# Linear attention and a channel mix on one core: the first load of q split by head pairs, zeros and a product moved ahead, and a new order of steps

## The chip, the cores and the metric

The kernel runs on 1 core of one Trainium2 chip. The metric is device time in microseconds. The median of three runs before the change is 200.35 us (200.12, 200.35 and 202.0).

## The reference, cut to what matters

Batch 8, 8 heads, 576 tokens, head size 64; so 512 channels, and 1024 in the hidden layer. Everything comes in as float32 and goes out as float32.

```
kv   = einsum('bhsd,bhse->bhde', k, v)            # 64x64 per head
out  = einsum('bhsd,bhde->bhse', q, kv)
rms  = sqrt(mean(out*out, axis=-1) + 1e-6)
x    = (out / rms * g_norm), heads side by side    # [8, 576, 512]
x_prev = x shifted by one token, zero at token 0
xk   = mu_k * x + (1 - mu_k) * x_prev              # xr alike with mu_r
k    = max(xk @ w_k, 0)                            # 512 -> 1024
v    = (k * k) @ w_v                               # 1024 -> 512
r    = sigmoid(xr @ w_r)                           # 512 -> 512
result = r * v
```

## The kernel before

The kernel works in bfloat16 with channels on the partitions. For each batch it forms k'v per head, turns q so that channels lie on partitions, multiplies the two into PSUM (`u`), squares the result on ScalarE, takes the mean over a head with a product by a block matrix on TensorE (`ms`), takes the inverse root on ScalarE (`rs`) and multiplies on VectorE (`mu`) into x. Then x_prev - x (`d`, for the first two batches `dc`), its products with 1 - mu (`sc`), and the sums xk and xr (`add`; `fu` does both in one step). Then come xk w_k (`K`), its relu out of PSUM (`Ko`) and its square (`ks`), xr w_r (`R`) with its sigmoid (`S`), the square times w_v (`V`, two halves), the product of both (`fin`) and the store (`st`). Pairs of batches share the buffers of xr and of the squares, so a 128-row tile of R and V covers 128 of 1152 tokens.

**The order is written out by hand.** All steps of all batches stand in one string, `ORDER`, of words like `uc.0.1=6`. The loop at the end of the kernel takes the words one after the other, looks the name up in a table (`ops`), and calls it with the numbers behind it; the digits after `=` are the PSUM banks that it takes (eight banks, 0 to 7); a trailing `'` puts a step that can run on VectorE or ScalarE on VectorE. Tile's scheduler is off (`tc.manual_schedule()`), so each engine runs its steps in the order of the string, and waits of one engine for another follow from the data and the buffers. The output buffers are a pool of six (`fin`, L601; `bufs=6`). The queues to know:

- POOL (GpSimd) issues every load that turns float32 into bfloat16: `lf` (a part of k, v or q of batch 0 or 1, L200; arguments batch, which of k v q as 0 1 2, head pairs from and to, columns from and to), `lw` (a part of w_k, w_r, w_v as 0 1 2, L221), `ld` (k, v or q of a later batch, L200, L212 and L214). `gt` copies one column of turned q, so that POOL waits until q of that batch has been turned.
- SP issues the first k and v of head pairs 0 and 1 without a cast (`lraw`, L188; then `cast`, L246 or L248, on ScalarE or VectorE), the rows of mu and g (`lrow`, L192 and L194), turns of q for batches 2 and on (`qd`, L362 and L364), turns of y for batches 5 and on (`yd`, L421) and the stores (`st`, L618).

**The front, batches 0 and 1.** `set.0` zeroes and fills small constants; `set.1` makes the identities; `set.2` writes zeros over the block forms of k'v (`kv_heads`, `kv_pairs`, L271), which batches 2 and on need. `wm.n` runs n products of zeros (L253), whose result nobody reads. `kc` (L302) is k'v for a range of head pairs, and `kco` its copy out of PSUM; `qc` (L313) turns q by products with the identity, `qco` copies it out (L246 or L248); `uc` (L324) multiplies a piece; `sq`, `ms`, `rs`, `mu` (L435, L439, L444, L463) are as above. Batch 0 is cut into seven pieces: 0, 1 and 2 are head pairs 0, 1 and 2 of columns 192 to 576, pieces 3 and 4 the two halves of these columns of head pair 3, and 5 and 6 the columns 0 to 192 of pairs 0 and 2, and of 1 and 3. `col` turns the rows of mu and g into columns (L467, L470, L471), which every `mu` and `sc` reads. `wrap` (L476) copies the last tokens of x ahead of the first ones. For batch 0 the product with w_k is done for the columns 256 to 576 first (`Kf`, one 128-channel block of the hidden layer and a range of head pairs, L531; `Kfo` out of PSUM), and for the columns 0 to 256 later (`Kl`, two blocks, L542; `Klo`). `ksp` squares parts of it. `tab` loads ScalarE's table for roots (0) or sigmoids (1).

In the order before, q of batch 0, columns 192 to 576 of all four head pairs, is one load, and the first on POOL's queue. The first word of the products with R comes ahead of `Kl`, and `set.2` comes after the last add of batch 0.

Of the kernel before, what the change touches and what calls it, by code (L numbers as in the profile page):

```python
# [30 lines left out]
    add.0.0.0.0.256 Kf.5.0.4.256=5 Kf.0.3.4.256 Kfo.0.256 Kfo.4.256 Kfo.5.256 lw.0.3.0.4.6.8 Kf.6.0.4.256=6
    Kf.7.0.4.256=1 Kfo.1.256' Kf.2.2.3.256 Kf.2.3.4.256 sc.0.0.3.0.256 Kfo.6.256 Kfo.7.256' add.0.0.1.0.256
    set.2 lf.1.2.0.4.0.576 qc.1.0.2.0.576=47 wm.2=5 qc.1.2.4.0.576=56 qco.1.1.0.576 qco.1.3.0.576 qco.1.2.0.576
    lw.1.0.0.4.0.4 R.0.1=0 R.0.0=7 S.0.0 Kfo.3.256' R.0.2=1 S.0.2 lf.1.0.0.4.0.576 R.0.3=6 S.0.3 Kfo.2.256'
    ksp.0.4.256.576' Kl.0.256=5 qco.1.0.0.576 Klo.0.256' Kl.3.256=3 Klo.3.256' lf.1.1.0.2.0.576 kc.1.0.2=27
    kco.1.1' lf.1.1.2.4.0.576 kc.1.2.4=16 kco.1.3' S.0.1 tab.0.1 kco.1.0 uc.1.1=4 ksp.4.8.256.576' kco.1.2'
    Kl.2.256=5 sq.1.1 ms.1.1=0 uc.1.5=3 uc.1.3=7 uc.1.2=2 sq.1.5 uc.1.0=6 Klo.2.256' ksp.4.8.0.256' rs.1.1
    mu.1.1 Kl.1.256=1 Klo.1.256' ksp.0.4.0.256' sq.1.3 sq.1.2 ms.1.5=5 rs.1.5 mu.1.5 sq.1.0 lw.2.0.0.4.0.4
    V.0.3.0=0 ms.1.2=4 rs.1.2 mu.1.2 ms.1.3=5 rs.1.3 mu.1.3 V.0.2.0=1 uc.1.4=4 sq.1.4 ms.1.0=3 rs.1.0 mu.1.0
    lw.2.1.4.8.0.4 V.0.3.1 ms.1.4=5 rs.1.4 mu.1.4 V.0.1.0=2 V.0.1.1 wrap.1 dc.1.0.2.0.576 V.0.2.1 ld.1.2  # L40
    dc.1.2.4.0.576 ld.0.2 sc.1.1.0' sc.1.1.3' V.0.0.0=3 V.0.0.1 sc.1.1.1 add.1.1.0 sc.1.1.2 add.1.1.1 R.1.6=7
    fin.0.2 sc.1.0.0 sc.1.0.2 ld.2.2 sc.1.0.3 sc.1.0.1 ld.2.3 fin.0.1 R.1.5=5 tab.1.1 S.1.5 kv.2=64 kvo.2.3
    qd.2.0 R.1.7=1 gt.2 add.1.0.0 add.1.0.1 K.1.3.1=2 K.1.2.0=5 fin.0.3 Ko.1.2.0' K.1.3.0=0 kvo.2.0' kvo.2.1'
    kvo.2.2 R.1.4=4 S.1.4 kvo.2.4' K.1.6.0=5 K.1.2.1=6 Ko.1.3.0' qd.2.1 qd.3.0 K.1.7.1=0 kvo.2.5' Ko.1.3.1'
    Ko.1.2.1' K.1.0.0=4 ks.1.2 K.1.7.0=2 R.1.8=6 fin.0.0 Ko.1.7.0' S.1.6 Ko.1.6.0 S.1.7 S.1.8 tab.0.2 st.0.2
    Ko.1.0.0' K.1.5.0=3 Ko.1.5.0' K.1.6.1=7 K.1.0.1=2 Ko.1.0.1 ld.1.3 Ko.1.7.1' ks.1.7' K.1.1.0=5 Ko.1.6.1
    ld.0.3 K.1.1.1=4 ld.0.4 Ko.1.1.0 Ko.1.1.1' ks.1.3' K.1.4.0=1 Ko.1.4.0 ld.1.4 K.1.5.1=6 u.2.1=30 u.2.2=2
    u.2.0=74 ld.2.4 ld.0.5 ld.1.5 ks.1.1' Ko.1.5.1' ks.1.5' ks.1.0 sq.2.3 sq.2.0 ks.1.6' K.1.4.1=5 Ko.1.4.1'
    ks.1.4' ms.2.3=1 rs.2.3 sq.2.2 mu.2.3 st.0.1 V.1.8.0=6 ms.2.0=5 V.1.8.1 sq.2.1 qd.3.1 ms.2.2=1 rs.2.0
    V.1.7.0=0 mu.2.0 rs.2.2 mu.2.2 fin.1.8 st.0.3 ms.2.1=5 rs.2.1 sq.2.4 V.1.4.0=1 V.1.6.0=7 mu.2.1 d.2.0 d.2.4  # L50
    ms.2.4=3 rs.2.4 mu.2.4 d.2.1 d.2.2 d.2.3 sc.2.1.0' qd.4.0 gt.3 sc.2.0.0 sc.2.0.2' sc.2.0.1' sc.2.1.1'
    V.1.7.1 add.2.1.0 V.1.5.0=5 V.1.5.1 sc.2.1.3 sc.2.1.2 tab.1.2 kv.3=64 kvo.3.3 kvo.3.1 kvo.3.0 kvo.3.2 gt.4
    V.1.6.1 qd.4.1 V.1.4.1 add.2.1.1 R.2.3=3 R.2.0=2 fin.1.5 fin.1.4 R.2.1=5 S.2.0 kvo.3.5 S.2.1 fin.1.6 st.1.8
    add.2.0.0 R.2.2=6 st.0.0 st.1.6 st.1.5 zl sc.2.0.3' kvo.3.4' S.2.3 add.2.0.1 fin.1.7 u.3.1=41 sq.3.2 kv.4=72
# [24 lines left out]
    ks.4.5' tab.1.5 mu.5.4 K.4.4.0=4 Ko.4.4.0' K.4.3.1=6 Ko.4.3.1' K.4.7.0=5 K.4.6.0=0 K.4.4.1=1 K.4.7.1=3
    K.4.6.1=7 ks.4.3 ks.4.1' V.4.1.0=4 V.4.3.0=6 Ko.4.4.1' Ko.4.7.0 Ko.4.7.1 kvo.6.5' ut.6.0=1 gs.5.0 kvr.6.0'  # L80
# [639 lines left out]
```

## Time and profile before

| what | us |
|---|---|
| median of 3 runs | 200.35 |
| the profiled execution, its own time | 200.72 |
| its span, first to last instruction | 198.9 |
| TensorE busy | 188.9 |
| VectorE busy | 156.7 |
| ScalarE busy | 144.5 |
| mean granted TensorE clock, as a share | 0.996 |
| first product with w_k (L531) starts | 17.08 |
| first product with w_r (L576) starts | 24.69 |
| first product with w_k of batch 1 (L556) starts | 45.5 |

The profiled execution is one run, recorded; its time of 200.72 us is its span and what lies around it. Times in the profile are from the start of the span. PE is TensorE's products, PEld its weight loads, DVE is VectorE, ACT ScalarE, POOL GpSimd, SP the sync engine. A line of a timeline gives the start, the length, the engine, the line of the kernel and the operation with what it writes and reads; in brackets stands how long the engine had been idle before it, and what ended that. A row of a group of equal instructions one behind the other is one line with its count. A chain of waits follows the work that ended last back to its start.

### The profile page before, as it was taken

The page shows a single profiled execution, that of the slowest core. Times are in us where ns is not written, and L with a number is a line of the kernel's source. Part 1 is how long each engine was busy: PE and PEld are TensorE (multiplying, and loading weights), DVE is VectorE, ACT ScalarE, POOL GpSimd, SP SyncE. Part 2 cuts the span into 40 slices and gives each one's busy share as a digit, 9 for nine tenths or more (in the row PEclk, how much of TensorE's full clock was granted, in tenths as well). Part 3 has the DMA queues.
Part 4 walks back from the last instruction along what each step waited for, and adds up shares of the span by engine and source line. Part 5 has one row for each costly group of instructions (what it writes and reads, how often), then busy time and mean ns, then how long its engine had stood idle before and what let it go on. Part 6 is the DMA issues. An engine that isn't in the chain of part 4 may idle for free.

```text
span 198.9 us, 4745 instructions
## 1 busy us (share of the span) xinstructions
PE 188.9 (95%) x1879; PEld 111.4 (56%) x1900; DVE 156.7 (79%) x348; ACT 144.5 (73%) x280; POOL 32.6 (16%) x54
## 2 busy tenths in 40 slices
PE   7879899999999999999999999999999999999991
PEld 2444556446745476545764477645764666476541
DVE  1259978998689988988799987996898788969242
ACT  3188868695995889989875997969798858528330
POOL 8485141001920000730005000000000000000000
PEclk9999999999999999999999999999999999999998
DMA  6999999999999999899997999519460126104154
GB/s 218 178 198 203 207 206 208 205 194 160 155 247 228 204 204 196 158 198 212 198 237 131 234 184 105 176 72 230 80 187 21 53 53 167 47 0 158 58 185 132
DMA packets 49547, 32.24 MB, mean 162 GB/s; under 512 B 25836, under 2 KB 44532, under 8 KB 49524
## 3 DMA queue, kind: packets, MB, share of 16 engines
q0 software_dynamic: 22672, 16.19, 54.8%
q1 hardware_dynamic: 26692, 15.61, 33.6%
q8 instruction: 15, 0.25, 0.5%
q10 hardware_dynamic: 160, 0.13, 0.3%
q14 instruction: 8, 0.07, 0.1%
HBM read 33.56 MB, written 9.44 MB: 216 GB/s over the span
## 4 chain that ended last, share of the span: by engine, by line
PE 70%; DMA 14%; DVE 9%; issue 2%; POOL 1%; ACT 1%; SPq 0%; POOLq 0%; DVEq 0%
PE ps_v L586 26%; PE ps_km L556 24%; PE ps_r L576 12%; DMA wr_sb<-in_moe_w_r_dram 6%; DMA out_dram<-out_sb 4%; DMA q<-in_q_dram 4%; DVE rt L520 3%; PE ps_km L542 2%; PE ps_ms L439 2%; DVE xT L463 2%; DVE xk L511 1%; PE ps_kv L338 1%; PE ps_u L392 1%; DVE out_sb L601 1%; PE ps_v L594 1%
## 5 line engine op out<-in xcount | busy, mean ns | idle before, releaser
L586 PE MATMUL ps_v<-wv_sb,sqk 128*128 128x512 bf16 x270 | 64.7, 379 | 0.8 <-issue 0.2
L556 PE MATMUL ps_km<-xk,wk_sb 128*128 128x288 bf16 x448 | 60.4, 286 | 0.1
L556 PEld LDWEIGHTS <-wk_sb 128*128 128x128 bf16 x448 | 43.2, 98 | 15.2 <-issue 0.8
L586 PEld LDWEIGHTS <-sqk 128*128 128x128 bf16 x280 | 26.9, 98 | 29.5 <-DVE sqk L526 0.9
L520 DVE TENSOR_SCALAR rt<-ps_km 128x288 bf16<-128x288 f32 (+2 forms) x65 | 29.1, 466 | 8.3 <-PE ps_km L556 6.2
L576 PE MATMUL ps_r<-wr_sb,xr 128*128 128x512 bf16 x136 | 32.8, 379 | 1.2 <-DMA wr_sb<-in_moe_w_r_dram 0.4
L601 DVE TENSOR_TENSOR out_sb<-ps_v,sig 128x512 f32<-128x512 f32 (+1 forms) x37 | 24.1, 669 | 8.3 <-PE ps_v L586 2.7
L518 ACT ACTIVATE rt<-ps_km 128x288 bf16<-128x288 f32 (+1 forms) x59 | 22.5, 410 | 10.3 <-PE ps_km L556 10.0
L581 ACT ACTIVATE sig<-ps_r 128x512 bf16<-128x512 f32 x36 | 20.9, 598 | 11.5 <-PE ps_r L576 7.1
L500 ACT ACTIVATE m<-dx,cols 128x576 bf16<-128x576 bf16 (+1 forms) x28 | 19.7, 757 | 6.2 <-DVE dx L483 2.6
L463 DVE SCALAR_TENSOR_TENSOR xT<-ps_u,cols,rs 128x512 bf16<-128x512 f32 (+4 forms) x31 | 19.0, 626 | 4.5 <-ACT rs L444 4.3
L576 PEld LDWEIGHTS <-xr 128*128 128x128 bf16 x144 | 13.6, 98 | 15.8 <-DVE xr L511 1.0
L444 ACT ACTIVATE rs<-ps_ms,eps 128x512 f32<-128x512 f32 (+4 forms) x31 | 18.2, 595 | 2.9 <-PE ps_ms L439 2.7
L648 ACT ACT_TABLE_LOAD x15 | 19.2, 1283 | 0.3
L526 DVE TENSOR_TENSOR sqk<-rt 128x576 bf16<-128x576 bf16 (+2 forms) x35 | 16.7, 488 | 1.7 <-ACT rt L518 0.9
L524 ACT ACTIVATE sqk<-rt 128x576 bf16<-128x576 bf16 x25 | 16.5, 680 | 1.6 <-DVE rt L520 1.3
L435 ACT ACTIVATE sq<-ps_u 128x512 bf16<-128x512 f32 (+4 forms) x31 | 14.8, 499 | 1.9 <-PE ps_u L324 0.8
L367 POOL COPY gates<-qT 128x1 bf16<-128x1 bf16 x5 | 1.3, 264 | 74.8 <-DMA qT<-in_q 74.8
L502 DVE TENSOR_SCALAR m<-dx,cols 128x576 bf16<-128x576 bf16 (+2 forms) x38 | 12.2, 364 | 0.2
L511 DVE TENSOR_TENSOR xk<-m,xT 128x1152 bf16<-128x1152 bf16 (+2 forms) x17 | 11.5, 696 | 0.7 <-ACT m L500 0.6
L511 DVE TENSOR_TENSOR xr<-m,xT 128x1152 bf16<-128x1152 bf16 x16 | 11.6, 752 | 0.4
L417 DVE TENSOR_TENSOR y<-ps_u,rst 128x512 bf16<-128x512 f32 x12 | 7.7, 685 | 3.9 <-ACT rst L410 3.9
(80 smaller groups left out, 171.7 us busy)
## 6 DMA issues: line engine op xcount, KB each, us to landing
out_dram<-out_sb SPq DMA_DIRECT2D x23, 256.0 KB, 2.3
in_k<-in_k_dram POOLq DMA_DIRECT2D x7, 576.0 KB, 14.7
in_v<-in_v_dram POOLq DMA_DIRECT2D x6, 576.0 KB, 13.4
in_q<-in_q_dram POOLq DMA_DIRECT2D x6, 512.0 KB, 16.1
out_dram<-out_sb SPq DMA_DIRECT2D x24, 128.0 KB, 3.1
wk_sb<-in_moe_w_k_dram POOLq DMA_DIRECT2D x4, 256.0 KB, 9.0
wv_sb<-in_moe_w_v_dram POOLq DMA_DIRECT2D x2, 512.0 KB, 16.7
sqk<-in_v_dram SPq DMA_DIRECT2D x1, 576.0 KB, 3.7
```

Of the source, the lines that this page charges most:

```text
L444: ACT.activation(out=rs[:, :ps.shape[1]], in_=ps, func=AF.Abs_reciprocal_sqrt, bias=eps)
L463: DVE.scalar_tensor_tensor(out=dst, in0=ps, scalar=g_sb, in1=rs, op0=ALU.mult, op1=ALU.mult)
L500: eng.activation(out=out_, in_=in_, func=AF.Copy, scale=mu)
L511: DVE.tensor_add(out=blended(a, which)[:, hs, c0:c1], in0=at[a]["m", which][:, hs, c0:c1], in1=xT[a % 2][:, hs, P + c0:P + c1])
L518: eng.activation(out=dst, in_=ps, func=AF.Relu)
L520: eng.tensor_scalar(out=dst, in0=ps, scalar1=0.0, scalar2=None, op0=ALU.max)
L556: nc.tensor.matmul(ps, wk_sb[:, cc, 128 * fc:128 * fc + 128], at[b]["xk"][:, cc, SH * h:SH * h + SH], start=(cc == 0), stop=(cc == NHP - 1))
L576: nc.tensor.matmul(ps, xr[:, cc, 128 * t:128 * t + 128], wr_sb[:, cc, :], start=(cc == 0), stop=(cc == NHP - 1))
L581: ACT.activation(out=sig[b, t], in_=give(("r", b, t)), func=AF.Sigmoid)
L586: nc.tensor.matmul(ps, sqk[:, fc, 128 * t:128 * t + 128], wv_sb[:, fc, :], start=(fc == 0), stop=(fc == NFC - 1))
L601: DVE.tensor_mul(out=o, in0=give(("v",) + key), in1=sig[b, t][:, c])
L648: "tab": lambda eng, n, b: ACT.preload_act_table_set(("abs_reciprocal_sqrt_and_small", "sigmoid_and_others")[n]),
```

## The change

Only the string `ORDER` changes; every function stays as it is. The work is the same but for the loads of q and the products of zeros:

- The load `lf.0.2.0.4.192.576` (four head pairs) becomes two, `lf.0.2.0.2.192.576` and `lf.0.2.2.4.192.576`, first and second on POOL's queue.
- `set.2` comes right after `set.0`, so VectorE writes these zeros at the start.
- `kc.0.0.2`, k'v of head pairs 0 and 1, comes ahead of `col.0`; its two copies change engines.
- Products of zeros: 12 + 7 ahead of the first k'v become 12 + 4; between the first k'v and the first `Kf` there were 7 and are 11; 2 + 2 later ones, among `Kf` and between the turns of q of batch 1, are gone.
- k and v of head pair 2 are loaded ahead of pair 3, and both ahead of the columns 0 to 192 of q; the parts of w_k come in the order 0, 1, 3, 2; w_r and k of batch 1 come ahead of q of batch 1.
- Of the pieces of batch 0, 2 comes ahead of 3 and 4. `Kl.3` and `Kl.2` come ahead of R.
- The order, the banks, and the choice of ScalarE or VectorE are new for the rest of the kernel too. On SP `qd.4.1` stands behind `st.1.8`, `st.0.0`, `st.1.6` and `st.1.5`, and `qd.6.0` ahead of `st.1.4`, `st.2.3` and `st.2.0`; on POOL q of batch 4 comes after k of batch 5.

The diff of the front, and of the later lines named here, cut to its core:

```
-    set.0 lraw.1 lraw.0 lrow wm.12=0 set.1 wm.7=1 col.0=1 cast.1 cast.0' kc.0.0.2=23 kco.0.0 lf.0.2.0.4.192.576
-    qc.0.0.2.192.576=45 qc.0.2.4.192.576=67 qco.0.2.192.576 col.1 kco.0.1' lf.0.1.3.4.0.576 qco.0.0.192.576'
-    uc.0.0=0 sq.0.0 qco.0.1.192.576' uc.0.1=1 sq.0.1 lf.0.0.3.4.0.576 kc.0.3.4=2 qco.0.3.192.576
-    lf.0.2.0.4.0.192 wm.1=3 ms.0.1=3 rs.0.1 ms.0.0=4 kco.0.3' uc.0.4=5 sq.0.4 mu.0.1 rs.0.0 mu.0.0 wm.1=6
-    qc.0.2.4.0.192=62 qc.0.0.2.0.192=73 qco.0.0.0.192' dc.0.0.2.256.576 uc.0.3=4 qco.0.1.0.192'
-    sc.0.0.0.256.576' sc.0.0.1.256.576' qco.0.2.0.192 ms.0.4=1 rs.0.4 sq.0.3 lf.0.1.2.3.0.576 lf.0.0.2.3.0.576
-    wm.1=6 kc.0.2.3=6 kco.0.2 ms.0.3=0 qco.0.3.0.192 uc.0.2=7 rs.0.3 mu.0.4 mu.0.3 sq.0.2 uc.0.6=1 sq.0.6
-    add.0.0.0.256.576 dc.0.3.4.256.576 fu.0.0.3.256.576 uc.0.5=6 sq.0.5 wm.2=3 ms.0.2=3 rs.0.2 mu.0.2
-    dc.0.2.3.256.576 fu.0.0.2.256.576 wm.2=2 ms.0.5=2 rs.0.5 mu.0.5 lw.0.0.0.4.0.2 Kf.1.0.2.256=0 ms.0.6=5
-    Kf.0.0.2.256=4 rs.0.6 wrap.0 lw.0.1.0.4.2.4 Kf.3.0.2.256=3 tab.1.0 mu.0.6 dc.0.0.4.0.256 sc.0.0.0.0.256'
-    sc.0.1.0 Kf.2.0.2.256=2 sc.0.1.2' sc.0.1.3' sc.0.0.2.0.256' add.0.1.1 sc.0.1.1 lw.0.2.0.4.4.6 wm.2=7
-    Kf.4.0.4.256=7 Kf.3.2.3.256 Kf.0.2.3.256 Kf.3.3.4.256 Kf.1.2.3.256 Kf.1.3.4.256 add.0.1.0 sc.0.0.1.0.256'
-    add.0.0.0.0.256 Kf.5.0.4.256=5 Kf.0.3.4.256 Kfo.0.256 Kfo.4.256 Kfo.5.256 lw.0.3.0.4.6.8 Kf.6.0.4.256=6
-    Kf.7.0.4.256=1 Kfo.1.256' Kf.2.2.3.256 Kf.2.3.4.256 sc.0.0.3.0.256 Kfo.6.256 Kfo.7.256' add.0.0.1.0.256
-    set.2 lf.1.2.0.4.0.576 qc.1.0.2.0.576=47 wm.2=5 qc.1.2.4.0.576=56 qco.1.1.0.576 qco.1.3.0.576 qco.1.2.0.576
-    lw.1.0.0.4.0.4 R.0.1=0 R.0.0=7 S.0.0 Kfo.3.256' R.0.2=1 S.0.2 lf.1.0.0.4.0.576 R.0.3=6 S.0.3 Kfo.2.256'
-    ksp.0.4.256.576' Kl.0.256=5 qco.1.0.0.576 Klo.0.256' Kl.3.256=3 Klo.3.256' lf.1.1.0.2.0.576 kc.1.0.2=27
-    kco.1.1' lf.1.1.2.4.0.576 kc.1.2.4=16 kco.1.3' S.0.1 tab.0.1 kco.1.0 uc.1.1=4 ksp.4.8.256.576' kco.1.2'
-    Kl.2.256=5 sq.1.1 ms.1.1=0 uc.1.5=3 uc.1.3=7 uc.1.2=2 sq.1.5 uc.1.0=6 Klo.2.256' ksp.4.8.0.256' rs.1.1
...
+    set.0 set.2 lraw.1 lraw.0 lrow wm.12=0 set.1 cast.1 cast.0' wm.4=1 kc.0.0.2=12 kco.0.0' kco.0.1
+    lf.0.2.0.2.192.576 wm.2=3 qc.0.0.2.192.576=34 qco.0.0.192.576' wm.2=5 uc.0.0=5 qco.0.1.192.576' uc.0.1=6
+    sq.0.0 lf.0.2.2.4.192.576 qc.0.2.4.192.576=70 qco.0.2.192.576' ms.0.0=1 lf.0.1.2.3.0.576 col.0=2 sq.0.1
+    qco.0.3.192.576 ms.0.1=3 rs.0.1 lf.0.0.2.3.0.576 kc.0.2.3=4 kco.0.2' wm.1=7 uc.0.2=7 rs.0.0 sq.0.2 col.1
+    mu.0.1 mu.0.0 wm.3=0 ms.0.2=0 lf.0.1.3.4.0.576 lf.0.0.3.4.0.576 lf.0.2.0.4.0.192 dc.0.0.2.256.576 kc.0.3.4=4
+    rs.0.2 kco.0.3' wm.1=3 uc.0.3=3 sq.0.3 uc.0.4=2 sc.0.0.0.256.576' mu.0.2 sc.0.0.1.256.576' qc.0.2.4.0.192=16
+    qco.0.2.0.192' qc.0.0.2.0.192=50 qco.0.1.0.192 ms.0.3=4 qco.0.3.0.192 qco.0.0.0.192' wm.2=7 uc.0.5=7 sq.0.4
+    rs.0.3 uc.0.6=1 sq.0.6 ms.0.4=0 rs.0.4 dc.0.2.3.256.576 add.0.0.0.256.576 fu.0.0.2.256.576 sq.0.5
+    lw.0.0.0.4.0.2 Kf.0.0.2.256=5 ms.0.6=6 rs.0.6 mu.0.3 mu.0.4 Kf.1.0.2.256=4 dc.0.3.4.256.576 lw.0.1.0.4.2.4
+    Kf.3.0.2.256=0 Kf.3.2.3.256 fu.0.0.3.256.576 ms.0.5=3 rs.0.5 tab.1.0 wrap.0 mu.0.6 mu.0.5 dc.0.0.4.0.256
+    sc.0.0.0.0.256' sc.0.1.0 sc.0.0.1.0.256' sc.0.0.2.0.256' sc.0.1.1' Kf.0.2.3.256 Kf.1.2.3.256 Kf.2.0.2.256=2
+    Kf.1.3.4.256 Kf.3.3.4.256 sc.0.1.3 Kfo.3.256 lw.0.3.0.4.6.8 add.0.0.0.0.256 Kf.0.3.4.256 Kfo.0.256
+    Kf.2.2.3.256 Kf.7.0.4.256=6 Kfo.7.256 lw.0.2.0.4.4.6 Kf.4.0.4.256=3 sc.0.0.3.0.256' add.0.0.1.0.256
+    Kf.5.0.4.256=1 add.0.1.0 Kf.6.0.4.256=7 Kf.2.3.4.256 sc.0.1.2 Kl.3.256=0 Klo.3.256 Kl.2.256=5 Kfo.1.256'
+    lw.1.0.0.4.0.4 add.0.1.1 R.0.1=6 S.0.1 Kfo.6.256 Kfo.4.256' Kfo.2.256' R.0.2=4 Kfo.5.256 Klo.2.256'
+    ksp.4.8.256.576' lf.1.0.0.4.0.576 R.0.3=0 S.0.3 R.0.0=3 Kl.0.256=2 Klo.0.256' S.0.2 S.0.0 tab.0.1
+    lf.1.2.0.4.0.576 qc.1.0.2.0.576=65 qco.1.1.0.576' qco.1.0.0.576 lf.1.1.0.2.0.576 kc.1.0.2=71 kco.1.0
+    kco.1.1' ksp.4.8.0.256' lf.1.1.2.4.0.576 qc.1.2.4.0.576=04 qco.1.3.0.576' uc.1.1=3 kc.1.2.4=25 sq.1.1
...
```

Later words, in order, of SP, of POOL, and of TensorE around batch 3 (other words left out):

```
SP before:   ... qd.4.0 qd.4.1 st.1.8 st.0.0 st.1.6 st.1.5 qd.5.0 st.1.4 st.2.1 qd.5.1 st.1.7 st.2.3 st.2.0 qd.6.0 yd.5.1 ...
SP after:    ... qd.4.0 st.1.8 st.0.0 st.1.6 st.1.5 qd.4.1 st.1.7 qd.5.0 qd.5.1 qd.6.0 st.1.4 st.2.3 st.2.0 yd.5.1 ...
POOL before: ... gt.2 ld.1.3 ld.0.3 ld.0.4 ld.1.4 ld.2.4 ld.0.5 ld.1.5 gt.3 gt.4 ld.1.6 ld.0.6 ld.2.5 ld.2.6 ld.0.7 gt.5 ld.1.7 ld.2.7 gt.6
POOL after:  ... gt.2 ld.1.3 ld.0.3 ld.1.4 ld.0.4 ld.0.5 ld.2.4 ld.1.5 gt.3 gt.4 ld.2.5 ld.1.6 ld.0.6 ld.2.6 ld.2.7 ld.0.7 gt.5 ld.1.7 gt.6
PE before, batch 3:  ... V.2.1.0=2 ms.3.4=3 V.2.0.0=1 V.2.3.0=5 V.2.3.1 V.2.1.1 V.2.0.1 u.4.1=04 u.4.0=37 R.3.7=6 ...
PE after, batch 3:   ... ms.3.4=2 V.2.1.0=4 V.2.0.0=3 V.2.3.0=5 V.2.0.1 V.2.3.1 V.2.1.1 u.4.0=20 u.4.1=71 R.3.6=6 ...
```

## The prediction

> **What bounds the kernel now.** I read the profiled page first, then busy time by stretches, then the timeline of the first 25 us, the waits of TensorE after that, and the chain of waits from 60 us on.
>
> ```profile
> PE 188.9 (95%) x1879; PEld 111.4 (56%) x1900; DVE 156.7 (79%) x348; ACT 144.5 (73%) x280; POOL 32.6 (16%) x54
> ```
>
> TensorE is busy for 95% of the span, but not all of that is useful. By stretches (length, then busy time of PE, weight load, DVE, ACT, POOL; granted clock; DMA share; GB/s):
>
> ```profile
> 17.00:24.70 7.70, 6.83 (x110) 4.48 (x112) 7.52 (x19) 6.41 (x13) 2.22 (x3) 1.00 1.24 207
> 24.70:45.00 20.30, 19.99 (x254) 10.77 (x258) 17.40 (x35) 15.84 (x28) 3.13 (x4) 1.00 1.31 203
> 45.00:194.40 149.40, 147.94 (x1323) 89.73 (x1338) 124.21 (x270) 113.38 (x222) 15.01 (x23) 1.00 0.81 151
> ```
>
> From 24.7 to 194.4 us TensorE idles 0.31 + 1.46 us: that part is TensorE's own work, the same before and after. What can move is the front, and the few waits later. The front, from the timeline (start, length, idle before in brackets):
>
> ```profile
> 1.20 6.77 PE L253 MATMUL ps_warm<-zeros 128*128 128x512 bf16 x19 [1.20 <-DVE eps L260]
> 9.38 0.58 PE L313 MATMUL ps_qt<-ident,q 64*64 64x64 bf16 x48 [0.70 <-DMA q<-in_q_dram]
> ...
> 11.36 0.23 DVE L248 CAST kvc<-ps_kv 128x64 bf16<-128x64 f32 x1 [0.93 <-PE ps_kv L302]
> 12.69 1.31 DVE L463 SCALAR_TENSOR_TENSOR xT<-ps_u,cols,rs 128x384 bf16<-128x384 f32 x2 [1.10 <-ACT rs L444]
> ...
> 15.76 0.48 DVE L511 TENSOR_TENSOR xk<-m,xT 128x640 bf16<-128x640 bf16 x1
> ...
> 17.08 0.43 PE L531 MATMUL ps_km<-xk,wk_sb 128*128 128x320 bf16 x2
> ...
> 24.80 1.03 DVE L271 MEMSET kvh<- 128x512 uint32 x2
> ```
>
> Dense useful work begins at 17.08, with the first w_k product (`Kf`). One wait of TensorE after 45 us, and one piece of the chain, matter besides:
>
> ```profile
> PE ps_r L576 <- DVE xr L511: 0.4, 1, 0.4
> ```
>
> ```profile
> 80.75 0.60 SPq L618
> 81.35 0.04 issue
> 81.40 8.32 DMA out_dram<-out_sb
> ...
> 89.82 0.13 DVE out_sb L601
> ```
>
> The last fence says that a store issued at 81.40 landed 8.32 us later, and that VectorE's output product (`fin.2.1`, which takes the buffer that `st.1.6` frees) and then batch 3's products waited for it. So time won early can be lost again there.
>
> **The change, part by part.** New times below are estimates, from durations of these rows.
>
> *Warm-ups.* Nineteen stand ahead of the first k'v, the first twelve 0.43 us apart (the weight loads at 1.60, 2.02, 2.45...), the rest 0.215. Sixteen end near 7.3 instead of 7.97, so k'v (0.48) runs 7.4 to 7.9; it ran 8.20 to 8.68. It needs both casts, ready at 6.81.
>
> *The split load.* The DMA view of 0 to 6.9 us has 0.22 MB on the software queue, that of 0 to 8 us 0.42: 192 KB are through at about 6.8, 384 KB at 7.9. The whole load landed at 9.33, 1.4 later, so the first half lands at 8.2: 1.1 earlier. One more issue costs POOL 0.56 to 0.89 us. POOL's waits show eight loads in flight (the ninth is issued at 9.62, after the first landed at 9.33); the eight hold 1.4 MB in the new order, 7 us at 203 GB/s, so the queue doesn't run dry and landings depend on bytes alone. Without that cover each later load would come 0.6 to 0.9 later.
>
> *To the first product.* Half of the transposes 8.45 to 8.8, their copies (0.35 each, 0.27 apart) to 9.5, two score pieces (0.35) to 9.9, two squares to 10.6, means (0.34) to 10.97, roots (0.58) to 11.6 and 12.1; the second root ended at 13.35. But on VectorE `kco.0.2'` now stands ahead of `col.1` and the two `mu`. It waits for k of head pair 2, which lands at 10.80 and whose products take 0.48; so it ends at 11.7, and behind it `col.1` (0.2) starts `mu.0.1` at 11.9, not at 11.6. Then in VectorE's order, with row durations: `mu` 1.2, diff 0.48, copy 0.23, scale 0.21, `mu.0.2` 0.62, scale 0.3, two copies 0.35, diff 0.32, add 0.48, with small gaps: the first xk is whole at 15.75 (16.24 before). TensorE had two means and four warm-ups ahead of `Kf` then and reached it 0.84 after xk; now only `ms.0.4`, done by then. `Kf` starts at 15.85: 1.2 earlier. Its weights landed at 15.1, so they don't stop it.
>
> *The w_k stream and what follows.* 32 products of 0.135 are 4.3 us; two means, and waits of about 0.2 for `sq.0.6` and 0.25 for `fu.0.0.3`, bring the end to 20.9 (22.4 before, with two warm-ups inside). A new wait then: `Kl.3` and `Kl.2` come ahead of R and need the low columns of xk, the end of a VectorE chain (wrap 0.22, two `mu`, diff 0.69, scales, adds) that I get to 21.9. TensorE idles 0.9, everything behind it too. Kl pair 1.75, so R begins at 23.55 (24.69 before). w_r lands at 21.3: its place in the queue moves ahead of 576 KB, 2.8 us by its landing at 24.56 less that of q at 21.48. At 23.55 two Kl are done that were not (1.75), and two blocks of transposes are not that were (0.95).
>
> *To batch 1.* Lead so far 1.14 + 1.75 - 0.95 = 1.9. q of batch 1 lands where k did (26.9) and is wanted at 27.9. v's second half lands at 29.7 as before, `kc.1.2.4` waits 0.2 for it, `ms.1.1` 0.25 for its square: lead 1.4 to 1.5. VectorE's chain to xr ends 1.5 earlier too (40.8, was 42.31), and R wants it at 41.1. I carry 1.4 us.
>
> *The zeros.* VectorE's memsets, 1.03 and 0.55, move from 24.80 to about 1.6, where it idled 4.45 us for raw k: nothing there; if raw k came 2.9 us sooner they would cost up to 1.6. At 24.80 no TensorE wait follows them, so leaving there brings nothing by itself.
>
> *Later order.* The 0.4 of R's wait for xr of batch 3 should close: `ms.3.4` now has six half V tiles behind it before R, not five (0.86 more). Elsewhere the order is new too, with the same work. I summed VectorE's and ScalarE's share of it with the row means: 4.3 and 2.6 us less than before after 45 us. Bounds for new small waits: nothing, to the 1.46 us that the old order had; I take 0.1 net, since loads and sums are no worse.
>
> *SP.* `qd.4.1` (1.62 us) now stands behind four stores, not ahead; q of batch 4 itself is loaded after k of batch 5 (lands about 74.6, was 71.3). Stores start near 78 to 79.5 (78.17 before), and `st.1.6` is through its issue about as far ahead of the next loads as its first half was before, which landed in time (issued 80.73, landed 84.44). I take no new cost, bound 0 to 2 us.
>
> **Sum.** 1.4 + 0.4 - 0.1 = 1.7 us. The profiled execution took 200.72 (span 198.9): it becomes 199.0. It stands 0.37 above the median of 200.35, so I forecast 198.6 as median.
>
> **Rivals.**
>
> *More is won.* The wait of 0.9 ahead of `Kl.3` and the 0.65 between w_k's landing and `Kf` are estimates of a VectorE chain of 20 steps; if it runs denser, most of both goes: 198.6 - 1.3 = 197.3. For it: VectorE's steps overlapped by 0.08 in several rows. Against: the mean of the rows is already packed.
>
> *The store takes it back.* Between 83.6 and 87.4 the hardware queue moved only 0.01 MB while the loads moved 0.59. If `st.1.6` is caught there again, batch 3's products start near 91.5 as before, and the lead shrinks to about 0.4: 200.0.
>
> *A split load pays its fixed time.* Two loads of 144 KB landed 0.72 apart, 200 GB/s, the rate of the big ones, so I see none. If each load in the queue held up the next, everything behind would come up to 2 us later: 200.6. The Trainium skill, "DMA: Bandwidth & Descriptors", section "Anatomy of one DMA", gives about 2 us of fixed time for each such transfer and advises large ones. By those landings it overlaps.
>
> *The clock falls back.* The first twelve warm-ups run at half the later rate. If TensorE were slow again through the first 3.4 us of `Kf`, that would be 1.7 us more: 200.3. Against: 0.70 was the longest gap and the pitch stayed 0.22; the new order has eleven warm-ups between k'v and `Kf`, not seven. The Trainium skill, "TensorE: Matmul & The Clock Gate", Part 1, says that an idle window of about 3.4 us halves the clock; no gap here is near it.
>
> *Slower: a turn of q holds the stores.* `qd.6.0` now stands on SP ahead of `st.1.4`, `st.2.3` and `st.2.0`. Its issue held SP for 6.78 us at 107.22. If q of batch 6 lands near 104, those stores are issued at 111 and land 2.3 later, at 113.3; `fin.3.7`, wanted at 108.5, needs the first one's buffer, and VectorE (9.52 of 10 us busy from 105 to 115) can't make up 4.8 us: 203.4. It loses to before once that landing is past 110.2. Against it: that q should land near 100, which puts the store at 109.
>
> **Chances.** Forecast 0.46, of which 0.20 lies below 198.35 (faster by over 1%); more won 0.20; the store 0.12; fixed time 0.03; clock 0.04; slower 0.15. One per cent is about what a measurement of this kernel can tell from no change. Faster 0.20 + 0.20 = 0.40; same 0.26 + 0.12 + 0.03 + 0.04 = 0.45; slower 0.15. The forecast's own range is 197.9 to 199.4. The range 197.0 to 201.0 takes in the fixed-time case and leaves out the slower case and little below.
>
> **What would show it.** Right: first transposes near 8.5, `mu.0.1` behind a wait for `kvc`, `Kf` before 16.3, a gap of TensorE ahead of the products of L542 near 21, R's first product (L576) near 23.6, K of batch 1 (L556) near 44 (45.5 now), no wait for xr near 86. Wrong: L531 still starting at 17, a gap of several tenths at L338 or L382, VectorE waiting for `out_dram` near 88 or 108, or warm-ups 0.43 apart after 8 us.

## The result, and the profile after

The changed kernel takes 208.0 us (median of six runs, 207.36 to 208.88); the kernel before, run beside it, 200.48 (six runs, 200.03 to 202.0). The ratio is 1.036 (95% interval 1.032 to 1.041): slower by 7.5 us, where 198.6 was forecast. Ratios here and below leave out a run that lies over 1.5% above the fastest of its kernel; medians take in all runs. The profiled execution took 208.46 us, with a span of 206.7 (198.9 before). In the changed kernel a line number is one lower than before: K of the later batches is L555, the output product (`fin`) L600, the store L617, and the turns of q L361 and L363.

The front did come earlier: K of batch 1 starts at 44.7 us instead of 45.35 (so the timeline of the kernel before; the 45.5 of the table above is from its chain of waits). The loss lies later, in two places. By stretches (start and end; length; busy time and instructions of PE, weight load, DVE, ACT, POOL; granted clock; DMA share; GB/s), the changed kernel, and then one stretch of the kernel before:

```profile
70.00:80.00 10.00, 5.25 (x105) 3.22 (x106) 4.89 (x12) 2.64 (x5) 0.00 (x0) 0.66 1.29 204
115.00:120.00 5.00, 4.49 (x22) 2.06 (x21) 3.21 (x7) 3.10 (x6) 0.00 (x0) 1.00 1.25 252
120.00:125.00 5.00, 3.96 (x37) 3.26 (x37) 4.43 (x8) 4.13 (x9) 0.00 (x0) 1.00 0.80 138
```

```profile
70.00:80.00 10.00, 10.00 (x203) 7.37 (x193) 8.11 (x20) 8.85 (x20) 0.05 (x1) 1.00 1.27 198
```

From 70 to 80 us TensorE is busy for 5.25 of 10 us, and at a granted clock of 0.66; before, it was busy for all 10 at 1.00. VectorE and ScalarE are idle for most of it too (4.89 and 2.64 busy), but the DMA share is as high as before (1.29 for 1.27), which points at a wait for a transfer. The second place, 115 to 125, costs 1.5 us. The waits (engine, what waited, line, for whom: us in total, times, longest), first TensorE's, then VectorE's:

```profile
PE ps_km L555 <- DVE xk L510: 7.0, 2, 5.4
```

```profile
DVE out_sb L600 <- DMA out_dram<-out_sb: 5.0, 2, 4.5
```

So TensorE waits twice for xk (5.4 and 1.6 us). Ahead of that xk VectorE waits (4.5 and 0.5 us) in a `fin`, for the landing of a store whose output buffer that `fin` is to take. Not all of the 5.4 is the store's: just ahead of that `fin` VectorE stood idle for 2.1 us in `kvo.3.2`, a copy of k'v that needs ScalarE's part first, so that without the store some 0.9 (5.4 less 4.5, an estimate) would have stayed. The chain of waits, cut to 48 to 80 us, says why the store was late (start, length, what):

```profile
48.61 0.28 SPq L617
...
48.93 0.58 SPq L617
...
49.61 7.30 SPq L361
...
57.01 2.91 SPq L363
...
59.97 0.58 SPq L617
...
60.61 12.63 DMA out_dram<-out_sb
...
73.33 0.69 DVE out_sb L600
74.02 0.67 DVE xk L510
...
74.74 0.66 PE ps_km L555 x2
...
75.41 2.56 PE ps_km L555 x10
```

Read it downwards. SP issues the store `st.0.1` (two transfers), and only then the turn `qd.3.0`, at 49.61. Its issue holds SP for 7.30 us, that of `qd.3.1` for 2.91. Behind them stands `st.0.3`; its second half leaves at 60.61 and lands 12.63 us later. `fin.1.7`, eighth to ask for one of six output buffers, gets that of `st.0.3`, the second store on SP, so it runs at 73.33, and both halves of xk of batch 2 stand behind it on VectorE. The last line is the second cost of the same wait: ten K products take 2.56 us, where ten of them take 1.2 elsewhere (eight in 0.98 at 99.97).

The kernel before had the same turns and stores in another order. SP's timeline of the kernel before, and then of the changed one (start, length, operation, count):

```profile
48.28 1.67 SPq L362 DMA_TRANSPOSE qT<-in_q  x1
50.05 3.32 SPq L618 DMA_DIRECT2D out_dram<-out_sb  x4
53.46 1.36 SPq L364 DMA_TRANSPOSE qTr<-in_qr  x1
54.92 1.20 SPq L618 DMA_DIRECT2D out_dram<-out_sb  x2
```

```profile
48.33 1.19 SPq L617 DMA_DIRECT2D out_dram<-out_sb  x2
49.61 7.30 SPq L361 DMA_TRANSPOSE qT<-in_q  x1
57.01 2.91 SPq L363 DMA_TRANSPOSE qTr<-in_qr  x1
59.97 2.52 SPq L617 DMA_DIRECT2D out_dram<-out_sb  x4
```

Before, `qd.3.0` left at 48.28, ahead of POOL's next loads, which `gt.2` lets go and whose first issue was at 49.18; its issue took 1.67 us, and the three stores of batch 0 that stand there were out by 56.1. One store of 1.2 us ahead of it moves it to 49.61, behind the first load's issue (49.55).

The chain of the changed kernel from 105 to 126 us shows the second place, of the same kind:

```profile
110.90 8.71 DMA out_dram<-out_sb
...
119.63 0.69 DVE out_sb L600
120.33 0.68 DVE xk L510
...
121.04 1.39 PE ps_km L555 x10
```

Here `st.2.3` has stood on SP behind `qd.6.0` (issued at 106.78, when its q had landed at 106.65) and `st.1.4`; it leaves at 110.90 and lands 8.71 us later, and `fin.3.5` waits 0.5 us for its buffer. The `fin` ahead of it, `fin.3.7`, takes the buffer of `st.1.4`. The second half of that store left at 110.22 and landed 8.2 us later, at 118.4; `fin.3.7` starts at 118.46, after 1.3 us of idleness. The list of waits puts these 1.3 us down to TensorE's R, which `fin.3.7` does not read, so by the times it was the store here too. This is the rival of the prediction that ended on the slower side.

The loss as a sum, from the profiled execution before: 200.72, less 0.7 of front, less 0.4 for the closed wait of xr, plus 5.4, plus about 1.75 for the twelve K products at the low clock (3.22 us instead of 1.47), plus 1.6: 208.4. The profile took 208.46. Only these terms are counted; that they close does not show that nothing else moved.

### The profile page after: what moved, and what is told of

The parts are those of the page before. It is cut to its first block, busy times and chain, and to the rows that moved or that the text cites. A ratio compares the mean times of both kernels' runs of the same rounds, so it can differ in the third digit from the quotient of the medians.

```text
span 206.7 us, 4772 instructions
## 1 busy us (share of the span) xinstructions
PE 191.5 (93%) x1897; PEld 112.2 (54%) x1897; DVE 155.7 (75%) x349; ACT 144.1 (70%) x279; POOL 33.7 (16%) x55
## 4 chain that ended last, share of the span: by engine, by line
PE 71%; DMA 10%; SPq 6%; DVE 6%; ACT 4%; issue 1%; ACTq 0%; DVEq 0%
PE ps_km L555 24%; PE ps_v L585 22%; PE ps_r L575 10%; DMA out_dram<-out_sb 10%; PE ps_warm L252 5%; SPq L361 4%; PE ps_ms L438 2%; PE ps_km L541 1%; PE ps_kv L337 1%; SPq L363 1%; DVE xT L462 1%; PE ps_u L391 1%; PE ps_u L323 1%; DVE out_sb L600 1%; PE ps_v L593 1%
## 5 line engine op out<-in xcount | busy, mean ns | idle before, releaser
L555 PE MATMUL ps_km<-xk,wk_sb 128*128 128x288 bf16 x448 | 61.8, 290 | 7.0 <-DVE xk L510 7.0
L555 PEld LDWEIGHTS <-wk_sb 128*128 128x128 bf16 x448 | 43.6, 99 | 21.8 <-DVE xk L510 5.9
L517 ACT ACTIVATE rt<-ps_km 128x288 bf16<-128x288 f32 (+1 forms) x72 | 27.2, 415 | 8.9 <-PE ps_km L555 8.6
L600 DVE TENSOR_TENSOR out_sb<-ps_v,sig 128x512 f32<-128x512 f32 (+1 forms) x37 | 24.2, 669 | 11.9 <-DMA out_dram<-out_sb 5.0
L519 DVE TENSOR_SCALAR rt<-ps_km 128x288 bf16<-128x288 f32 (+2 forms) x52 | 23.3, 467 | 10.2 <-PE ps_km L555 8.5
L580 ACT ACTIVATE sig<-ps_r 128x512 bf16<-128x512 f32 x36 | 20.4, 598 | 10.6 <-PE ps_r L575 8.3
L499 ACT ACTIVATE m<-dx,cols 128x576 bf16<-128x576 bf16 x29 | 20.5, 765 | 5.7 <-DVE dx L490 2.7
L525 DVE TENSOR_TENSOR sqk<-rt 128x576 bf16<-128x576 bf16 (+2 forms) x39 | 18.2, 482 | 6.3 <-ACT rt L517 6.0
L523 ACT ACTIVATE sqk<-rt 128x576 bf16<-128x576 bf16 x21 | 13.6, 681 | 1.2 <-DVE rt L519 1.0
L438 PE MATMUL ps_ms<-sq,means 128*128 128x512 bf16 (+4 forms) x31 | 10.0, 333 | 1.2 <-ACT sq L434 1.2
L252 PE MATMUL ps_warm<-zeros 128*128 128x512 bf16 x27 | 9.9, 508 | 1.2 <-DVE eps L259 1.2
## 6 DMA issues: line engine op xcount, KB each, us to landing
in_q<-in_q_dram POOLq DMA_DIRECT2D x6, 512.0 KB, 18.2
```

Source lines behind the costliest of these rows:

```text
L252: nc.tensor.matmul(ps, zeros[:, :128], zeros, start=True, stop=True)
L499: eng.activation(out=out_, in_=in_, func=AF.Copy, scale=mu)
L517: eng.activation(out=dst, in_=ps, func=AF.Relu)
L519: eng.tensor_scalar(out=dst, in0=ps, scalar1=0.0, scalar2=None, op0=ALU.max)
L555: nc.tensor.matmul(ps, wk_sb[:, cc, 128 * fc:128 * fc + 128], at[b]["xk"][:, cc, SH * h:SH * h + SH], start=(cc == 0), stop=(cc == NHP - 1))
L580: ACT.activation(out=sig[b, t], in_=give(("r", b, t)), func=AF.Sigmoid)
```

## The experiments

Theory S: the order of words on SP lost the time, in two places. Against it stood theory F (the new front costs, and later waits only show it) and theory L (the loads are late or in the way by themselves). An edit moves words of `ORDER` only, unless it says otherwise.

**One store behind the turns.** The first place mended by itself.

```
- qd.2.0 qd.2.1 st.0.1 qd.3.0 qd.3.1 st.0.3 st.0.2      (SP's order, changed kernel)
+ qd.2.0 qd.2.1 qd.3.0 qd.3.1 st.0.1 st.0.3 st.0.2
```

> One word of the changed kernel moved: the store st.0.1 stands behind qd.3.1 on SP instead of ahead of qd.3.0. Theory S (the order on SP lost the time): qd.3.0 leaves in the gap before POOL's loads start and its issue takes under 3 us instead of 7.30; st.0.3 lands before 66 instead of at 73.2; VectorE's wait of 4.5 us for a store and TensorE's wait of 5.4 us for xk go, and with them the ten K matmuls that took 2.56 us at half rate where they take 1.2 (some 1.9 us in all at the low clock). 208.0 - 5.4 - 1.9 = 200.7, range 200.0 to 202.0. Theory L (the loads of the software queue are late or in the way by themselves, wherever the store stands): the wait for xk stays over 3 us and the time over 205. Theory F (the new front cost it, later waits only show it): within 1 us of 208.

Four runs: 201.06, 207.34, 207.38 and 207.42 us (the kernel before beside it: 200.47, median of 13). The profile is of 207.34; none of the short run is kept, so what that run did without is not shown. In the profile the first place is mended as theory S said: `qd.3.0` leaves at 48.29 and takes 3.13 us, the last store of batch 0 has landed by 64.1, and TensorE is busy 9.75 of 10 us from 70 to 80. But the second place now costs more. Its chain from 84 to 126 us (line numbers are five lower in this kernel):

```profile
107.91 7.92 DMA out_dram<-out_sb
...
115.85 0.69 DVE out_sb L595
116.54 0.68 DVE xk L505
...
117.26 2.56 PE ps_km L550 x10
```

The store lands at 115.83, 3.8 us earlier than in the changed kernel; but TensorE, freed of the first wait, is there 6 us earlier and waits 3.9 us instead of 1.6, and then runs at a clock of 0.60 (115 to 120) and 0.72 (120 to 125). So the first half of theory S holds in this profile; my range (200.0 to 202.0) takes in one run of four and fails in three. In the three the two places do not add up. By this profile, and by that of the run with the loads held back, below, the first wait had been covering most of the second.

**The same order put into the kernel before.**

```
- qd.2.1 qd.3.0 st.0.2 st.0.1 qd.3.1 st.0.3      (SP's order, kernel before)
+ qd.2.1 st.0.2 qd.3.0 qd.3.1 st.0.1 st.0.3
```

> The kernel before with two words moved: qd.3.0 and qd.3.1 stand behind the store st.0.2 and ahead of st.0.1 on SP, as a store and the two turns stand in the changed kernel; the front is untouched. Theory S: qd.3.0's issue takes about 7 us and qd.3.1's 3, st.0.1 and st.0.3 leave after 59 and land near 73, fin.1.6 waits for the buffer of st.0.1 from 67 to 73, and TensorE loses 4 to 6 us and then some 2 us at the low clock: 200.5 + 6 to 8 = 206.5 to 208.5, at least 204. Theory F and L: 199.5 to 201.5.

Measured: 204.25, 205.37, 207.91 and 208.35 us, median 206.64; the ratio, from the two shorter runs, is 1.019 (1.010 to 1.028). With the front of before untouched, two moved words on SP make a loss of the same kind: some 4 us by the ratio, 8 in the longest run, which is the one profiled, so its size is not settled. SP's timeline in that run, and VectorE's wait (line numbers are six lower here):

```profile
48.48 1.18 SPq L612 DMA_DIRECT2D out_dram<-out_sb  x2
49.76 10.23 SPq L356 DMA_TRANSPOSE qT<-in_q  x1
60.09 2.83 SPq L358 DMA_TRANSPOSE qTr<-in_qr  x1
63.02 1.18 SPq L612 DMA_DIRECT2D out_dram<-out_sb  x2
```

```profile
DVE out_sb L595 <- DMA out_dram<-out_sb: 6.8, 1, 6.8
```

So the loss does not need the new front. That the new front does not cost it either shows below, where both places are mended and the front stays.

**Seven output buffers.** One number: `bufs=6` becomes `bufs=7` in `finish`; the order is that of the changed kernel.

> The changed kernel with 7 buffers for out_sb instead of 6, its order untouched. Theory S with the buffer as the last link: qd.3.0 still takes about 7 us and st.0.3 still lands near 73, but fin.1.7 takes the buffer of st.0.1 (landed at 52) and no longer stands ahead of the two halves of xk; fin.1.4 behind them then waits for st.0.3 until about 73, so that some of the loss may stay on VectorE. The 5.4 us shrink to 0 to 2.5: 201 to 205. Theory L (late loads or transposes stop TensorE, not the buffer): 207 to 208.5.

Measured: 206.4 us, ratio 1.027 (1.021 to 1.032): below my 207 to 208.5 for theory L, but above the 201 to 205 for theory S. The waits of 60 to 85 us (line numbers are six lower):

```profile
DVE out_sb L594 <- DMA out_dram<-out_sb: 3.6, 1, 3.6
...
PE ps_u L375 <- DVE kvh L241: 3.2, 1, 3.2
```

`fin.1.7` no longer waits and xk passes; `fin.1.4`, next on VectorE, now waits for the same late store, and the copies of k'v behind it are what TensorE lacks. One more buffer moves the wait by one `fin`: the buffer is only where the late store is felt.

**Both places mended.**

```
- qd.2.1 st.0.1 qd.3.0 qd.3.1 st.0.3          - qd.5.1 qd.6.0 st.1.4 st.2.3 st.2.0
+ qd.2.1 qd.3.0 qd.3.1 st.0.1 st.0.3          + qd.5.1 st.1.4 st.2.3 qd.6.0 st.2.0
```

> The changed kernel with st.0.1 behind qd.3.1, and qd.6.0 behind st.2.3 instead of three stores ahead of it. Theory S: as with st.0.1 moved alone, and the store whose landing at 119.6 held fin.3.7 and then xk (TensorE idle 1.6 us at 119.5 to 121.0, 1.9 us in 110 to 125) leaves some 2 us earlier, so 1 to 2 us less than with st.0.1 moved alone: 198.8 to 200.2. Rival: the front's new order is worth nothing, or the stores are held by something else: no less than with st.0.1 alone, 200.5 or more.

Measured: 200.27 us (ten runs, 199.94 to 201.05), ratio 0.998 (0.996 to 1.001). Two words on SP give back all of the 7.5 us. They leave the change at no gain that can be measured, 0.07 us over the upper end of my range.

**The second place mended alone.** Only `qd.6.0` is moved.

> The changed kernel with qd.6.0 alone moved behind st.1.4 and st.2.3 on SP; st.0.1 stays ahead of qd.3.0. Theory S with two places that add up: the 5.4 us and the low clock near 70 stay, the 1.9 us of 110 to 125 go: 206.1, range 205.3 to 207. If the second place is only the echo of the first: 208.

Measured: 207.5 us, ratio 1.034 (1.029 to 1.040); 0.5 over the range. The second wait is gone (TensorE busy 9.61 of 10 us from 110 to 120, 9.95 from 120 to 130), the first is longer in this profile, 6.6 us. So each of the two places can cost nearly the whole loss when it stands alone: about 7 us here, and as much in three of the four runs with the first place mended.

**The second place put into the kernel before.**

```
- qd.5.0 st.1.4 st.2.1 qd.5.1 st.1.7 st.2.3 st.2.0 qd.6.0      (SP's order, kernel before)
+ qd.5.0 qd.5.1 qd.6.0 st.1.4 st.2.1 st.1.7 st.2.3 st.2.0
```

> The kernel before with qd.5.1 and qd.6.0 moved ahead of st.1.4 on SP, as they stand in the changed kernel. Theory S: q of batch 6 lands near 98 here, the turns hold SP until about 109 instead of 100.9, st.1.4 and those behind it leave 8 us later, fin.3.7 and its neighbours wait for their buffers, and TensorE loses 2 to 6 us: 202.5 to 207. If stores may come late there without harm: 200.0 to 201.0.

Measured: 206.25 us (four runs, 204.74 to 208.05), ratio 1.025 (1.018 to 1.031), inside my 202.5 to 207. The chain from 95 to 125 us:

```profile
108.93 8.10 DMA out_dram<-out_sb
...
117.12 0.69 DVE out_sb L601
...
118.88 0.76 DVE xk L511
```

TensorE is busy 6.36 of 10 us from 110 to 120 (9.89 in the kernel before). The turns let go of SP at 106.5, not at 109 as I had it; the store lands 8.10 us after its issue. In this profile the front was late too, by 1.3 us (K of batch 1 at 46.7), which belongs to the run and not to the edit: TensorE's granted clock was 0.50 from 11.4 to 18.2 us, where it was 1.00 in the kernel before.

**Is it the loads?** The stores stay as the change has them. Only POOL's gate for the turn of batch 3 moves up, so that POOL holds its loads until `qd.3.0` has landed:

```
- gt.2 ld.1.3 ld.0.3 ld.1.4 ld.0.4 ld.0.5 ld.2.4 ld.1.5 gt.3 gt.4     (POOL's order)
+ gt.2 gt.3 ld.1.3 ld.0.3 ld.1.4 ld.0.4 ld.0.5 ld.2.4 ld.1.5 gt.4
```

> The changed kernel as it is, with st.0.1 ahead of qd.3.0, but POOL's gate for the turn of batch 3 moved up behind that turn, so that POOL issues the loads of batches 3 to 5 only when qd.3.0 has landed. It tells whether the loads make the issue of qd.3.0 long or its place behind a store does. Loads: qd.3.0 is issued at 49.6 in under 2.5 us, the stores st.0.3 and st.0.2 leave before 56 and land before 66, the wait of 5.4 us near 70 goes, and the loads start 3 to 5 us later, which may cost at 75 to 85; 200.5 to 204 with the second place left as it is, or up to 207 if that place answers as it did when st.0.1 alone was moved. Place behind a store: qd.3.0 still takes 7 us, 208 or more.

SP's timeline:

```profile
48.22 1.87 SPq L617 DMA_DIRECT2D out_dram<-out_sb  x2
50.19 1.97 SPq L361 DMA_TRANSPOSE qT<-in_q  x1
52.27 1.70 SPq L363 DMA_TRANSPOSE qTr<-in_qr  x1
54.01 2.51 SPq L617 DMA_DIRECT2D out_dram<-out_sb  x4
```

Behind the store, and even later than in the changed kernel (50.19), the turn is issued in 1.97 us once no load is in flight; the last store of batch 0 lands at 61.9, and TensorE is busy 9.75 of 10 us from 70 to 80. The loads make the issue long, not the place behind a store. The time, 208.43 us (four runs, 206.82 to 209.63; ratio 1.036, 1.031 to 1.041), lies above my range. In the profile, which is of 206.82, the second place answers with a wait of 4.7 us, as it did when `st.0.1` alone was moved; what made the other three runs longer is not shown.

**The front alone.** The changed kernel's order up to R of batch 1, then the order of before.

> The changed kernel's order up to the point where xr of batch 1 is ready (just ahead of R of batch 1), then the order of the kernel before for all that is left, on every engine and queue; the banks of PSUM are given anew behind the join. It has the split load, the moved zeros and the new front, and none of the later order. If the front is worth what K of batch 1 showed (44.75 for about 45.4) and nothing takes it back: 200.5 - 0.7 = 199.8, range 199.3 to 200.3. If it is worth the forecast 1.4: 199.1. If it is lost again at the late store of batch 1 (the rival that the store takes it back): 200.3 to 200.8. If the front costs (theory F): over 201.

Measured: 201.23 us (before beside it 200.85), ratio 1.002 (0.999 to 1.005): no gain. By the time alone it would fall to theory F (over 201), but the kernel before took 0.35 more beside it than I had reckoned with, and the interval takes in 1. The first w_k product is at 15.72 and K of batch 1 at 44.28, 1.1 us ahead of before; but K of batch 2 is at 70.91, for 70.92 before. The lead is lost at the join itself: from 44 to 60 us TensorE is busy 14.92 of 16 us (15.89 before), waiting for VectorE ahead of the first K (0.4) and for ScalarE's sigmoids (0.7). Another 1.1 us goes at 115, where xk of batch 4 waits behind a `fin` and that `fin` 1.5 us for a store: the second place again, though the words stand there as before. As a measure of the front this run is inconclusive, since the join is mine.

**The split load undone,** in the kernel with both places mended: `lf.0.2.0.4.192.576` instead of the two halves.

> The changed kernel with the two SP words mended (200.27 in four rounds' runs), and the first piece of q in one load again instead of two. If the split is what brings the first transposes forward (8.98 against 9.38): they start near 9.4 again and the time rises by 0.2 to 0.5, to 200.5 to 200.8. If k of head pair 2 on VectorE sets the front and not q: no change, within 0.2 of 200.3. If two loads cost a fixed time on the queue: faster by up to 1.

Measured: 200.93 us, 0.13 over the 200.5 to 200.8 for a useful split, ratio 1.001 (0.999 to 1.004); with the split it was 0.998 (0.996 to 1.001), measured at another time. The sign is that of a useful split, but the intervals touch. The traces say more. TensorE's timeline with the first products of k'v, the first transposes and the first w_k product, with one load, and then with two (line numbers are five lower in the second):

```profile
6.90 0.48 PE L301 MATMUL ps_kv<-rt 64*64 64x64 bf16 x36
9.02 0.38 PE L312 MATMUL ps_qt<-ident,q 64*64 64x64 bf16 x24 [1.11 <-DMA q<-in_q_dram]
...
16.60 0.43 PE L530 MATMUL ps_km<-xk,wk_sb 128*128 128x320 bf16 x2
```

```profile
6.93 0.48 PE L296 MATMUL ps_kv<-rt 64*64 64x64 bf16 x36 [0.46 <-DVE rt L242]
8.10 0.38 PE L307 MATMUL ps_qt<-ident,q 64*64 64x64 bf16 x24
...
15.67 0.44 PE L525 MATMUL ps_km<-xk,wk_sb 128*128 128x320 bf16 x2
```

With equal k'v (6.90 and 6.93) the split brings the transposes from 9.02 to 8.10, and the first w_k product follows them in both by 7.6 us.

**One more word moved.** In the kernel with both places mended TensorE still waited 1.1 us for xk of batch 2: VectorE stood 2.1 us in a copy of k'v (`kvo.3.2`) that needs ScalarE's part first, with `fin.1.7` and xk behind it. The edit puts the copy behind xk:

```
- kvo.3.3 kvo.3.2' fin.1.7 add.2.0.0 ... add.2.0.1
+ kvo.3.3 fin.1.7 add.2.0.0 ... add.2.0.1 kvo.3.2'
```

> The changed kernel with the two SP words mended, and the copy kvo.3.2 moved behind the second half of xk of batch 2 on VectorE. In the kernel with the two words mended VectorE stood idle for 2.1 us at 65.3 to 67.5, waiting for ScalarE's part of that copy, with fin.1.7 and both halves of xk queued behind it, and TensorE idled 1.1 us at 68.2 to 69.8 for xk. If that is the cause: the wait for xk goes and the time is 200.3 - 1.1 = 199.2, range 198.8 to 199.7. If xk's wait only moves (to the copies that the next products need): 200.0 to 200.5.

Measured: 199.53 us (twelve runs, 198.86 to 201.74; before beside it 200.89), ratio 0.994 (0.991 to 0.998). It is inside the range, and the interval lies below 1, but 0.6% is less than the one per cent that the prediction takes for what a measurement of this kernel can tell. Against the kernel with both places mended (0.998) the intervals touch. The wait for xk of batch 2 is gone from the profile. That profile is of one of its longer runs, 201.19 us: there VectorE waits 2.1 us for a store ahead of a `fin` at 89.7, and TensorE 1.8 for that `fin`, which is the prediction's rival that the store takes the lead back.

**Fewer warm-ups.** The same with 13 products of zeros ahead of the first k'v instead of 16 (`wm.4=1` becomes `wm.1=1`).

> The same, with 13 warm-up products ahead of the first k'v instead of 16. In seven profiled runs of the new front the first w_k product came 8.7 us behind the first k'v in six, and k'v began at 6.93 where the warm-ups' pitch fell from 0.43 to 0.22 us by 5 us, at 7.5 to 7.8 where it fell past 6. With 13 the warm-ups end by 6.8 even at 0.43 each, so k'v always begins near 6.95: no profile later than 7.1, and the mean of the runs 0 to 0.6 below the kernel with 16: 198.8 to 199.6. Rival: with fewer products the clock's step comes later, in useful work, and the time rises by 0.2 to 1.

Measured: 199.97 us (198.97 to 201.88), ratio 0.995 (0.992 to 0.997), the same as with 16 and 0.4 over my range. Its one profile, of 198.97 us, has k'v at 6.78, as expected; no gain in the time shows. It has no wait of VectorE for a store: TensorE is busy 9.95 of 10 us from 80 to 90, where the profile of 201.19 us has 8.30.

## Why the prediction was wrong

**The step that failed** is the part on SP: "I take no new cost, bound 0 to 2 us." It looked at `qd.4.1`, which costs nothing that the traces show, and not at `st.0.1`, which the change puts ahead of `qd.3.0`. The row was there: the kernel before issued `qd.3.0` at 48.28 in 1.67 us, and POOL's loads at 49.18. Of `qd.4.1` the prediction asks what its issue takes (1.62 us); of no word does it ask which deadline stands behind. Behind `st.0.1` (1.2 us) stood one, the start of the loads. The price is 5.4 us of wait, 4.5 of it the store's, and 1.75 of clock.

**The slower rival was right in its mechanism, and near in its price by luck.** It named `qd.6.0` ahead of `st.1.4`, `st.2.3` and `st.2.0`, and `fin.3.7` waiting. I held against it that q of batch 6 should land near 100; it landed at 106.65. And I let the stores land 2.3 us after their issue; those that mattered took 8.71, 7.92 and 8.10 us, with loads of the software queue in flight. The prediction's own first pages had the number: `st.1.6`, 8.32 us. Put alone into the kernel before, this place costs 5.4 us by the medians (206.25 for 200.85), and the rival had 4.8. But the store that mattered there left at 108.93, not at 111, and landed 8.10 us later, not 2.3: two errors that nearly cancel. The rival had a chance of 0.15, and its 203.4 holds nothing for the first place.

**Later order, "0.1 net".** The wait of R for xr closed, as forecast: 0.4 gained. But the bound for new waits, 1.46 us, was what the old order had had. That is no bound for a new order. Besides the two places, a wait for xk of 1.1 us (seen with both places mended) was of this kind, from the copy `kvo.3.2`.

**The front: right in kind, and near in size.** Forecast: first transposes 8.45, first w_k product 15.85, a gap ahead of `Kl` of 0.9, R at 23.55, K of batch 1 at 43.95, lead 1.4. The changed kernel's profile: 8.98, 16.56, 0.70, 24.45, 44.7, lead 0.7. The nine profiles with the new front have the transposes at 7.94 to 8.98 when q comes in two loads, and K of batch 1 at 43.4 to 44.7: leads of 0.7 to 1.9 over the 45.35 of before. The limit there was not the one of the forecast. The first half of q landed at 7.7 in the changed kernel, ahead of the 8.2 of the forecast, and in all nine profiles the transposes start 1.16 to 1.19 us behind k'v, but anywhere from 0.04 to 1.4 us behind the landing of q. When k'v starts is decided by the warm-ups, at one point that I had fixed at twelve slow ones:

```profile
1.20 6.47 PE L252 MATMUL ps_warm<-zeros 128*128 128x512 bf16 x16 [1.20 <-DVE eps L259]
7.82 0.48 PE L301 MATMUL ps_kv<-rt 64*64 64x64 bf16 x36
```

```profile
1.20 5.28 PE L247 MATMUL ps_warm<-zeros 128*128 128x512 bf16 x16 [1.20 <-DVE eps L254]
6.93 0.48 PE L296 MATMUL ps_kv<-rt 64*64 64x64 bf16 x36 [0.46 <-DVE rt L242]
```

These are the first products of the changed kernel and of the one with both places mended. The same sixteen products take 6.47 us and 5.28, because their pitch falls from 0.43 to 0.22 us at about 6.9 in the one and at 4.6 in the other. In the second, k'v waits for its cast (VectorE's, done at 6.88), in the first for the warm-ups.

The long chain that I worked out behind the transposes was hardly the point. The first w_k product follows the first transposes by 7.57 to 7.73 us in the profiles of the new front, and by 7.70 and 7.73 in two of the old one (by 9.6 in the third, the one whose front was late). Up to that product all of the front's gain is the earlier transposes; the new order behind them is worth about 0.1. From there to K of batch 1 it takes 27.8 to 28.6 us in the nine and 28.3 and 28.5 in the two, so some tenths more are won there in most of them, 0.7 at the most.

**The zeros** cost and bring nothing: the memsets run at 1.7 to 3.3 us, before the raw k lands, as forecast. **A fixed time of the split load** is not seen. **The clock** did not fall back in the front of any profile of the new order; in the changed kernel it fell in the 5.4 us of idleness. In one profile of the old front, that of the second place put into the kernel before, it did: TensorE was busy for 1.82 us of the 3.42 from 7.99 to 11.41, its longest gap was 1.49, and the granted clock was then 0.50 to 18.2. The first w_k product came at 18.94 there, not at 17.08. So the rival was real, and what I held against it, that the gaps are short, does not rule it out.

The Trainium skill, "TensorE: Matmul & The Clock Gate", Part 1, says that an idle window of about 3.4 us halves the clock, and that this window runs free, so that the change comes at another point in each run. The traces agree with it in that K runs at 0.24 us each after 5.4 us of idleness and after 3.9, not after 1.6, and that the warm-ups' change of pitch comes anywhere from about 4 to 7 us. They differ in that a stretch busy for more than half was enough, in the one profile just named.

**What stays open.** Where the front's lead of 0.7 to 1.9 us at batch 1 goes in the end: mended, the change is worth 0.9 and 1.4 us by the medians of its two forms (0.5% and 0.6% by the ratios), of which the earlier xk of batch 2 and the closed wait of xr are a part. No run separates them. Two profiles point at the store near 89 us: with a wait of 2.1 us for it the time is 201.19, without it 198.97. They are one run each, of kernels that differ by three warm-ups, so it is not shown. Nor do the traces show why a turn's issue is held while loads are in flight, only that it is.

## What to carry to other kernels

Where a queue issues both stores and loads or turns, each word moved on it has a deadline behind it: list for each the next traffic that it must be ahead of, and read the issue time and the landing time of a transfer from rows with the same traffic in flight, not from the median. Waits in two places need not add up: a first one can cover a second, so that mending one alone can show almost nothing; mend both, or put each into the kernel that lacks it. A wait taken as "at most what the old order had" is no bound for a new order.

## What the runs showed of the hardware that was not expected

- How long the issue of one and the same turn of 512 KB holds SP depends on the loads of the software queue. `qd.3.0` took 1.67 and 3.13 us when it was issued 0.9 and 1.0 us ahead of POOL's first load (48.28 for 49.18, 48.29 for 49.25), and 7.30, 8.98, 9.46 and 10.23 us when it was issued 0.06 to 0.4 us behind it (49.61 for 49.55, 49.70 for 49.36, 49.74 for 49.41, 49.76 for 49.39). With the loads held back it took 1.97 us at 50.19. So one microsecond of place on the queue decides over 4 to 8.6.
- A store of 128 or 256 KB issued into such a stretch lands 8 to 13 us later (8.10, 8.71, 12.63); the medians in the profile before were 3.1 for stores of 128 KB and 2.3 for 256 KB.
- TensorE's granted clock fell to 0.50 behind a stretch of 3.42 us in which it had been busy for 1.82, with no gap over 1.49 (the kernel before with the second place put in). It stayed at 1.00 behind stretches of 3.41 us that were busy for 2.61 and 2.69 (the kernel before).
